# One core, delta rule plus gated feed-forward: grams 7, 10 and 11, a mask and the weight parts in other places of the order

## The chip, the cores and the metric

The program runs on one core of one Trainium2 chip, in one launch. Its time is the device time in microseconds (us); where several runs are given, it is their median. Times inside an execution are counted from the first instruction of the profiled one. The five engines are called PE (matrix multiplies, with PEld for its weight loads), DVE (vector), ACT (scalar), POOL and SP; SP and POOL issue most of the DMAs.

## The reference

Two stages stand behind each other. The first is a delta rule over 768 tokens for 4 batches and 8 heads of width 48:

```
for t in range(S):
    kt, vt, bt = (k_n[:, :, t], v[:, :, t], beta[:, :, t, None])
    y[:, :, t] = np.einsum('bhd,bhde->bhe', q[:, :, t], state)
    v_old = np.einsum('bhde,bhd->bhe', state, kt)
    state = state + bt[:, :, :, None] * np.einsum('bhd,bhe->bhde', kt, vt - v_old)
```

`k_n` is k divided by its norm. The second stage takes y as tokens of width 384: `h = gelu(x @ w_in)` (1024 wide), halves u and v, v normalised over its 512 columns, mixed over the tokens by `w_sg`, gated with u, multiplied by `w_out` and added to x.

## The kernel before

The tokens are cut into 12 chunks of 64 per pair of batches. For each chunk c the kernel needs a gram (products of k with k and of k with q, PE, copied by ACT into the tile `gm`), the inverse of a triangular matrix made from it (tile `zl`), and then the chain of the chunk. The inverse is made for two segments of two chunks at once by `lanes(g)`: g=0 is segment 0, g=1 segment 1, g=2 segments 2 and 3, g=3 segments 4 and 5. The gram is stored to memory by four small DMAs (`gstore`, tile `gd`), loaded in another layout (`zload`, tile `zl`), and worked on by about two hundred small DVE instructions. The result is stored (`zstore`, tile `zd`) and fetched per chunk (`zfetch`, tiles `zk` and `z`).

The chain of a chunk runs in turns, listed in `TURNS` as pairs (chunk, feed-forward chunk): turn 0 is (0, -), turn 1 (1, -), turn 2 (2, 0), turn 3 (3, 1), turn 4 (-, 2), turn 5 (4, 3), then (5, 4) to (11, 10) and (-, 11). The index of the turn is `at`. In a turn PE does old0, own0, state0, old1, own1, state1 and gram; between them stand pieces of the feed-forward of another chunk (gate, values), and at the end the two corners of the next chunk, which need its `z` and, from DVE, `vprep` (L481) and `turned` (L442). old0 and old1 end in a DVE addition (L508), on which own0 and own1 wait.

The order on every engine is the order of the code (`manual_schedule`); each engine takes its list from the front. Only the long DVE work is spread: `bg` is a list of closures with estimated costs, and `tick` takes some off after each piece, by the share of the turn in `SHARE`. In `bg` stand the operations of `lanes` and the parts of the decoding of `w_in`: per piece k three parts, begin, middle and end (`b`, `t`, `e` below), on ACT (L582, L583, L593) and DVE (L584 to L600). A piece is loaded into one of three buffers `ut` by `win_load`; the end of piece 1 issued the load of piece 4.

In turns 0 and 1 no feed-forward stands beside the chain. There `fill` takes its places: gram 6 in turn 0, gram 7 in turn 1, each in two halves, after some empty places (`later_on`). After the second half of gram 7 come its stores, the loads of `zl` for segments 2 and 3, and `lanes(2)` is put into `bg`. In turn 4 grams 10 and 11 (`dense`) and their stores stand together near the turn's end; the loads of `zl` for segments 4 and 5 follow, and `lanes(3)` goes into `bg` after own1 of turn 5.

After turn 11 a second phase with dense matrix multiplies (L639 to L641 with `wsgh` and `wouth`) fills PE to the end.

Of the kernel before, what the change touches and what calls it, by code (L numbers as in the profile page):

```python
# [23 lines left out]
NCH = SEQ // T  # L24
# [6 lines left out]
NC = DM // P  # L31
# [10 lines left out]
N_LAST = 4  # L42
# [13 lines left out]
def delta_rule_gmlp_kernel(  # L56
# [13 lines left out]
    nc = tc.nc  # L70
# [61 lines left out]
    def load(q, tile, src):  # L132

        flat = tile.rearrange("p j t -> p (j t)") if len(tile.shape) == 3 else tile.rearrange("p i j t -> p (i j t)")
        q.dma_start(
            out=flat.rearrange("p (n x) -> p n x", x=src.shape[-1]), in_=src.rearrange("n p x -> p n x"))

    loads = [nc.sync]

    def kload(c):  # L140
        if c < NCH:
            load(loads[0], KD[c % N_2], kqT[c])
# [9 lines left out]
    def vload(c):  # L152
        if c < NCH:
            load(loads[0], V[c % N_2], vtok[c])

    bg, credit = [], [0.0]
# [73 lines left out]
    def gstore(c, queues):  # L230
        if c >= NCH:
            return
        s, c2 = c // 2, c % 2
        if c2 == 0:
            gdt[s] = dram.tile([2, 2, 2, NP, 32, 32], F32, name="gd", bufs=4)
        for half in range(2):
            for sd in range(2):
                r0 = 64 * sd + 32 * half
                queues[(half + sd) % len(queues)].dma_start(
                    out=gdt[s][half, sd, c2].rearrange("j s t -> s j t"),  # L240
                    in_=GM[c % N_M][r0:r0 + 32, :, 0, 32 * half:32 * half + 32],
                )
# [8 lines left out]
    def above(c):  # L251

        if c >= NCH:
            return
        m = GM[c % N_M][:, :, 1]
        nc.vector.tensor_tensor(out=m, in0=m, in1=later.unsqueeze(1).broadcast_to([P, NP, T]), op=ALU.mult)
# [20 lines left out]
    def gram(c):  # L277

        if c >= NCH:
            return [[]] * 4  # L280

        def phase(qd):
            st = {}
            js = slice(4 * qd, 4 * qd + 4)

            def step(h):
                if h == 0:
                    st["ps"] = bank().rearrange("p (j x t) -> p j x t", x=2, t=T)
                for sd in range(2):
                    kq = KD[c % N_2][OWN[sd], :, 4 * qd + h]  # L290
                    mm(st["ps"][TOK[sd ^ (qd // 2)], h], kq[:, 0], kq)

            def done():
                nc.scalar.copy(out=GM[c % N_M][:, js], in_=st["ps"])

            return step, done, 4

        return [[phase(qd)] for qd in range(4)]

    def zload(s):  # L300
        if s >= NSEG:
            return
        if s % 2 == 0:
            zsrc[0] = prep.tile([P, 2, 32, 32], F32, name="zl")
        nc.sync.dma_start(
            out=zsrc[0][:, s % 2], in_=gdt.pop(s).rearrange("a b c j s t -> (a b c j) s t"))
# [270 lines left out]
    def decode(raw, f, m, hv, lv):  # L577
        low, top = raw[:, :, 0], raw[:, :, 1]
        mf, ff, lowf = m.bitcast(F32), f.bitcast(F32), raw.bitcast(F32)[:, :, 0]

        def one():
            nc.scalar.activation(out=mf, in_=raw.bitcast(F32)[:, :, 1], func=AF.Abs)  # L582
            nc.scalar.copy(out=lowf, in_=low.bitcast(U32))  # L583
            nc.vector.tensor_scalar(  # L584
                out=f, in0=top, scalar1=3, scalar2=0x3FFFFFFF,
                op0=ALU.logical_shift_left, op1=ALU.bitwise_and)
            nc.vector.scalar_tensor_tensor(
                out=f, in0=top, scalar=-0x40000000, in1=f, op0=ALU.bitwise_and, op1=ALU.bitwise_or)

        def two():  # L590
            nc.vector.scalar_tensor_tensor(
                out=ff, in0=mf, scalar=LEAST, in1=ff, op0=ALU.is_ge, op1=ALU.mult)
            nc.scalar.copy(out=hv, in_=ff)  # L593
            nc.vector.tensor_scalar(out=m, in0=f, scalar1=-0x800000, scalar2=None, op0=ALU.bitwise_and)
            nc.vector.scalar_tensor_tensor(
                out=lowf, in0=lowf, scalar=2.0 ** -52, in1=mf, op0=ALU.mult, op1=ALU.mult)

        def three():
            nc.vector.tensor_tensor(out=ff, in0=ff, in1=hv.bitcast(F32), op=ALU.subtract)
            nc.vector.tensor_tensor(out=lv, in0=lowf, in1=ff, op=ALU.add)  # L600

        return one, two, three
# [7 lines left out]
    def win_load(k, q):  # L610
        raw = fw.tile([P, 2, ND, 2, T], F32, name="ut", bufs=3).rearrange("p a b c d -> p (a b c d)")
        raw = raw.bitcast(I32)
        q.dma_start(out=raw.rearrange("p (n x) -> p n x", n=2), in_=w_in[k].bitcast(I32).rearrange("n p x -> p n x"))
        wraw[k] = raw.rearrange("p (n x) -> p n x", x=2)

    def decode_win(k):
        kk, cols = PIECES[k]
        parts = []

        def begin():  # L620
            f = fw.tile([P, DH], F32, name="vg", bufs=4)
            m = fw.tile([P, DH], F32, name="vg", bufs=4)
            parts.extend(decode(
                wraw.pop(k), f.bitcast(I32), m.bitcast(I32), winh[:, kk, cols], winl[:, kk, cols]))
            parts[0]()

        def end():
            parts[2]()
            win_left.remove(k)
            if 4 <= k + 3 < 2 * NC:  # L630
                win_load(k + 3, loads[0])

        win_left.append(k)
        return [(begin, 1.1), (lambda: parts[1](), 1.9), (end, 1.4)]
# [181 lines left out]
        deal([k0], [k1])  # L816
        gstore(c, (nc.sync, nc.scalar))
    nc.scalar.dma_start(out=beta_l, in_=beta)
    (b0, t0, e0), (b1, t1, e1), *others = [decode_win(k) for k in range(2 * NC)]
    win = [b0, b1, t0, e0, t1]  # L820
    waiting = [e1]
    for begin, *rest in others:
        win += [begin, *waiting]
        waiting = rest
    win += waiting
    zload(0)
    for _ in range(N_EARLY):
        win.pop(0)[0]()
# [2 lines left out]
    def dense(c):  # L831
        g = gram(c)
        deal(g[0], g[2])
        deal(g[1], g[3])

    def values_of(c):
        q0, q1 = qgram(c)
        deal([q0], [q1])
# [23 lines left out]
    kload(6)  # L862
    for k in (2, 3):
        win_load(k, nc.sync)
    bg += lanes(1) + win
    above(0)
    vprep(0)
# [26 lines left out]
    for at, (c, f) in enumerate(TURNS):  # L894
        new = at + N_GRAMS if at <= N_LAST else NCH
        ch = chain(c, new if at > 1 else NCH) if c is not None else None
        fill = []

        def rest(g, new, at):
            deal(g[1], g[3])  # L900
            gstore(new, (nc.sync,))
            if at == 1:
                zload(2)
                zload(3)
                bg.extend(lanes(2))

        if at < 2:
            g = gram(new)
            later_on = [lambda: None] * (4 - 2 * at)
            fill = [*later_on, lambda g=g: deal(g[0], g[2]), lambda g=g, new=new, at=at: rest(g, new, at)]  # L910
        after = TURNS[at + 1] if at + 1 < len(TURNS) else (None, None)
        n = after[0]
# [3 lines left out]
        def spent(what, n=1):  # L916
            tick(per * n * COST[what])

        def does(name):
            if ch:  # L920
                ch[name]()
                spent(name)

        def feeds(name, *i):
            if ffn:
                getattr(ffn, name)(*i)
                spent(name, i[0] if name == "values" else 1)
            elif fill:
                fill.pop(0)()
# [6 lines left out]
        def unit():  # L936
            if units:
                units.pop(0)()

        def early():  # L940
            k = next((k for k, _ in TURNS[at + 1:] if k is not None), None)
            if k is not None and k not in zks and k // 2 in zds:
                zfetch(k, nc.sync)
# [24 lines left out]
            units = [v_unit] * NT  # L968
        if c is not None:
            vload(c + 1)  # L970
        kload(new + 1)
        does("old0")
        early()
        if n is not None:
            if n > 1:
                above(n)
# [2 lines left out]
        feeds("gate", 0)  # L979
        does("own0")  # L980
        unit()
        feeds("gate", 1)
        early()
        does("state0")
# [5 lines left out]
        does("old1")  # L990
        unit()
        feeds("values", 4)
        does("own1")
        if c == 4:
            bg.extend(lanes(3))
        if c is not None:
            tload(c + 1)
        if ch and n is not None and n not in zks:
# [18 lines left out]

        if n == 1:
            values_of(n)
            above(n)  # L1020
        if ch:
            ready()
            corner("corner_a")
# [6 lines left out]
            spent("turn")  # L1030
        does("gram")
        if at > 1:
            if not ch:
                dense(new)
            gstore(new, (nc.sync,))
            if at == N_LAST:
                dense(new + 1)
                gstore(new + 1, (nc.sync,))
        if ffn:
            feeds("values", 2)  # L1040
        if ch:
# [11 lines left out]
        if n == 4:  # L1053
            zload(4)
            zload(5)
        if f == NK - 1:
            bg.extend(norm(0))
        if c == NCH - 4:
# [120 lines left out]
```

## Time and profile before

| what | value |
|---|---|
| runs | 537.33, 535.11, 536.76 us; median 536.76 |
| the profiled execution | 534.14 us, span 532.4 us |
| granted clock, mean | 0.871 of full speed |
| busy | PE 438.7 us (82%), PEld 396.1, DVE 331.8 (62%), ACT 181.9, POOL 71.6 |
| chain that ended last | PE 62%, DVE 19%, DMA 8%, ACT 5%, issue 5% |

How to read it: a busy engine at the bottom of the chain counts only in the stretch where it is the last to be ready. The mean of PE, 82%, hides stretches with nothing on PE and a second phase without a gap. "Issue" is idle time for which the profile shows no releaser. The granted clock of PE has two levels, 1.2 GHz (0.5) and 2.4 GHz (1.0).

### The profile page before, as it was taken

The numbers are of one execution on the slowest core, as the hardware profiler recorded it, in microseconds if no ns is written. First come the engines' busy times: TensorE is split into PE (matmuls) and PEld (weight loads), VectorE is DVE, ScalarE is ACT, GpSimd is POOL, SyncE is SP. The second block draws the span as 40 slices with busy tenths as digits, with TensorE's granted clock in tenths as the row PEclk, the third lists the DMA queues.
The fourth block names the chain that finished last, engine by engine and source line by source line (L and its number), as shares of the span: only waits on it lengthen the run. The fifth ranks groups of instructions, "written<-read, shape, count | busy, mean of one in ns | idle before, by whom it ended". The sixth has DMA issues, their size and how long they took to land.

```text
span 532.4 us, 17771 instructions
## 1 busy us (share of the span) xinstructions
PE 438.7 (82%) x7679; PEld 396.1 (74%) x7679; DVE 331.8 (62%) x932; ACT 181.9 (34%) x411; POOL 71.6 (13%) x84
## 2 busy tenths in 40 slices
PE   4414674825979989899949998999998999999997
PEld 2413664815858878787748787888998999999996
DVE  2999968849992227889913458633699536623332
ACT  3323244423333534153324455544434212211110
POOL 2100010040010203011010110000034222322130
PEclk9577555556988979899988997999999999999999
DMA  7996799276194986574594779456937654244204
GB/s 183 262 225 146 177 292 274 39 194 173 52 269 143 281 226 151 151 245 121 185 234 108 229 188 252 129 169 184 289 120 205 189 155 136 74 148 149 78 12 133
DMA packets 109181, 92.79 MB, mean 174 GB/s; under 512 B 71600, under 2 KB 84848, under 8 KB 109104
## 3 DMA queue, kind: packets, MB, share of 16 engines
q1 hardware_dynamic: 99152, 69.41, 46.6%
q0 software_dynamic: 5600, 20.71, 14.2%
q10 hardware_dynamic: 4352, 1.54, 1.2%
q8 instruction: 60, 0.98, 0.8%
q14 instruction: 17, 0.14, 0.1%
HBM read 63.30 MB, written 28.34 MB: 172 GB/s over the span
## 4 chain that ended last, share of the span: by engine, by line
PE 62%; DVE 19%; DMA 8%; ACT 5%; issue 5%; SPq 1%; ACTq 1%; DVEq 0%
PE ps L82 19%; PE ps L639 12%; PE ps L641 11%; PE ps L640 11%; PE ps L675 8%; DVE ztmp L367 4%; DVE zl L374 3%; DMA vraw<-vD 2%; DMA z<-zd 2%; DMA ut<-w_in 1%; DMA zl<-gd 1%; DMA kd<-kqT 1%; PE ps L661 1%; DVE vraw L754 1%; DVE bs L687 1%
## 5 line engine op out<-in xcount | busy, mean ns | idle before, releaser
L82 PEld LDWEIGHTS ps<-s,kq 48*64 48x64 f32 x1408 | 54.6, 157 | 16.0 <-issue 8.9
L82 PE MATMUL ps<-s,kq 48*64 48x48 f32 x1408 | 61.2, 243 | 4.2 <-issue 2.9
L782 POOL TENSOR_TENSOR ga<-ga,uT 128x384 f32<-128x384 f32 x32 | 36.3, 1141 | 162.9 <-DVE ga L779 117.6
L82 PE MATMUL ps<-kd 48*64 48x128 f32 (+1 forms) x768 | 33.8, 321 | 25.0 <-DMA kd<-kqT 25.0
L367 DVE TENSOR_TENSOR ztmp<-zl 128x50 f32<-128x50 f32 (+22 forms) x208 | 53.6, 296 | 0.1
L374 DVE TENSOR_TENSOR zl<-zl,ztmp 128x50 f32<-128x50 f32 (+22 forms) x208 | 53.4, 295 | 0.0
L82 PEld LDWEIGHTS ps<-kd 48*64 48x64 f32 x768 | 29.5, 169 | 27.2 <-DMA kd<-kqT 14.9
L82 PE MATMUL ps<-v,z 64*64 64x48 f32 x768 | 35.2, 247 | 16.8 <-issue 6.4
L639 PE MATMUL ps<-xh,winh 128*128 128x256 f32 x144 | 47.5, 330 | 0.6 <-issue 0.6
L82 PEld LDWEIGHTS ps<-v,z 64*64 64x64 f32 x768 | 31.8, 161 | 18.3 <-issue 10.2
L640 PE MATMUL ps<-xl,winh 128*128 128x256 f32 x144 | 43.4, 302 | 1.8 <-DVE xl L665 1.0
L641 PE MATMUL ps<-xh,winl 128*128 128x256 f32 x144 | 43.1, 299 | 0.8 <-issue 0.8
L644 ACT CAST gh<-ga 128x384 fp32r<-128x384 f32 x32 | 16.4, 511 | 77.3 <-POOL ga L782 63.5
L687 DVE BATCH_NORM_STATS2 bs<-vg 128x6 f32<-128x512 f32 x24 | 16.6, 690 | 29.9 <-ACT vg L681 29.7
L645 DVE TENSOR_TENSOR gl<-ga,gh 128x384 fp32r<-128x384 f32 x32 | 18.1, 565 | 26.8 <-ACT gh L644 26.8
L82 PE MATMUL ps<-u,gm 64*64 64x48 f32 x768 | 32.5, 239 | 2.7 <-issue 2.1
L641 PE MATMUL ps<-wouth,gl 128*128 128x384 f32 x96 | 32.4, 340 | 1.5 <-DVE gl L645 1.5
L639 PE MATMUL ps<-wsgh,vnh 128*128 128x384 f32 x96 | 32.6, 340 | 0.1
L641 PE MATMUL ps<-wsgh,winl 128*128 128x384 f32 x96 | 32.5, 339 | 0.0
L639 PE MATMUL ps<-wsgh,winh 128*128 128x384 f32 x96 | 32.5, 339 | 0.0
L640 PE MATMUL ps<-wsgl,winh 128*128 128x384 f32 x96 | 32.5, 339 | 0.0
L640 PE MATMUL ps<-wsgl,vnh 128*128 128x384 f32 x96 | 32.5, 339 | 0.0
(122 smaller groups left out, 1070.2 us busy)
## 6 DMA issues: line engine op xcount, KB each, us to landing
kq<-kqT POOLq DMA_DIRECT2D x10, 896.0 KB, 9.0
uD<-ut SPq DMA_DIRECT2D x12, 512.0 KB, 6.2
vD<-vg SPq DMA_DIRECT2D x24, 256.0 KB, 4.5
vraw<-vD SPq DMA_DIRECT2D x48, 128.0 KB, 3.2
uT<-uD SPq DMA_DIRECT2D x8, 768.0 KB, 5.1
kd<-kqT SPq DMA_DIRECT2D x6, 896.0 KB, 9.3
xD<-x SPq DMA_DIRECT2D x12, 384.0 KB, 6.7
x<-xD SPq DMA_DIRECT2D x48, 96.0 KB, 2.6
```

The lines of the kernel that those rows point to most:

```text
L82: return nc.tensor.matmul(out=out, lhsT=lhsT, rhs=rhs, start=start, stop=stop, skip_group_check=True)
L367: tv.tensor_tensor(out=st["tmp"][:, at:at + (r1 - r0) * w].rearrange("p (r t) -> p r t", t=w), in0=z[:, a, r0:r1, i:i + 1].broadcast_to([P ...
L374: tv.tensor_tensor(out=z[:, a, r0:r1, i + 1:32], in0=z[:, a, r0:r1, i + 1:32], in1=st["tmp"][:, at:at + (r1 - r0) * w].rearrange("p (r t) ...
L639: nc.tensor.matmul(out=ps, lhsT=sh, rhs=mh, start=(first and i == 0), stop=False)
L640: nc.tensor.matmul(out=ps, lhsT=sh, rhs=ml, start=False, stop=False)
L641: nc.tensor.matmul(out=ps, lhsT=sl, rhs=mh, start=False, stop=(last and i == n - 1))
L644: nc.scalar.copy(out=hi, in_=src)
L645: nc.vector.tensor_tensor(out=lo, in0=src, in1=hi.bitcast(F32), op=ALU.subtract)
L661: nc.tensor.transpose(out=ps[:, cc], in_=x[:, cc * P:(cc + 1) * P], identity=ident)
L675: nc.tensor.matmul(out=self.ps, lhsT=(self.xl if k == 2 else self.xh)[:, cc, bi], rhs=(winl if k == 1 else winh)[:, cc, DH:], start=(i == ...
L687: nc.vector.bn_stats(out=bs, in_=self.vg[bi])
L782: nc.gpsimd.tensor_tensor(out=gv, in0=gv, in1=uT[:, :, d], op=ALU.mult)
```

## The change

No arithmetic changes; instructions move.

- Turn 1: no empty places before gram 7; its halves stand after old0 and after own0 (before: after state0 and after old1). Its stores, the loads of `zl` and `lanes(2)` move with it.
- The mask of chunk 1 (`above(1)`, DVE L256) moves from the end of turn 0 to turn 1, behind old0.
- The parts of the `w_in` pieces come in another order: the end of piece 1 is done before the turns, the load of piece 4 is issued at the start of turn 0 and not by that end, and later ends stand ahead of the next middle part.
- Turn 4: gram 10 with its stores stands behind the first gate, gram 11 behind the second group of values (before both near the end). The k of chunk 11 is loaded at the end of turn 3 rather than at the start of turn 4.
- `lanes(3)` goes into `bg` at the end of turn 4, not after own1 of turn 5.

```
-            if 4 <= k + 3 < 2 * NC:
+            if 5 <= k + 3 < 2 * NC:
                 win_load(k + 3, loads[0])
...
+    win = [b0, b1, t0, e0, t1, e1, b2, t2, b3, e2, t3, b4, e3, t4, b5, e4, t5, e5]
...
     for k in (2, 3):
         win_load(k, nc.sync)
+    win.pop(0)[0]()
     bg += lanes(1) + win
...
-            later_on = [lambda: None] * (4 - 2 * at)
+            later_on = [lambda: None] * (4 - 4 * at)
...
-        kload(new + 1)
+        if at < N_LAST:
+            kload(new + 1)
+        if at == 0:
+            win_load(4, loads[0])
         does("old0")
         early()
+        if c == 1:
+            above(c)
...
+        if at == N_LAST:
+            dense(new)
+            gstore(new, (nc.sync,))
         feeds("gate", 1)
...
         feeds("values", 4)
+        if at == N_LAST:
+            dense(new + 1)
+            gstore(new + 1, (nc.sync,))
         does("own1")
-        if c == 4:
-            bg.extend(lanes(3))
...
+            if at == N_LAST - 1:
+                kload(NCH - 1)
...
             zload(4)
             zload(5)
+            bg.extend(lanes(3))
```

ACT in turn 1, before. `gm7` is the tile of gram 7; L582 and L583 begin a weight piece, L593 is in its middle part.

```order
L582 ACTIVATE vg_1265<-ut_1149 128x512
L583 CAST ut_1149<-ut_1149 128x512
L543 COPY s1_110<-ps_117 112x384
L558 COPY x_1303<-ps_1227 128x384
L593 CAST winh_69<-vg_1189 128x512
L294 COPY gm7_101<-ps_1312 128x512
L294 COPY gm7_101<-ps_1315 128x512
L593 CAST winh_69<-vg_1264 128x512
L294 COPY gm7_101<-ps_1354 128x512
L294 COPY gm7_101<-ps_1357 128x512
```

The same place now, from the first copies of gram 7:

```order
L294 COPY gm7_101<-ps_1229 128x512
L294 COPY gm7_101<-ps_1232 128x512
L530 COPY u_106<-ps_1252 128x384
L593 CAST winh_69<-vg_1192 128x512
L582 ACTIVATE vg_1289<-ut_1148 128x512
L583 CAST ut_1148<-ut_1148 128x512
L294 COPY gm7_101<-ps_1294 128x512
L294 COPY gm7_101<-ps_1297 128x512
L543 COPY s1_110<-ps_117 112x384
L558 COPY x_1359<-ps_1249 128x384
```

The last copies of gram 7 stood behind the middle part of piece 5; now they stand behind the middle part of piece 4 and the beginning of piece 5.

DVE at the start of turn 5, before: the corner's work for chunk 4, the two additions of its turn (L508), then the first instruction of `lanes(3)` (L322), which reads the loaded `zl`.

```order
L442 STREAM_TRANSPOSE ztk<-zk 128x256
L508 TENSOR_TENSOR v_107<-v_107,ps 128x384
L256 TENSOR_TENSOR gm_99<-gm_99,later 128x16x64
L508 TENSOR_TENSOR v_107<-v_107,ps 128x384
L322 COPY d_2864<-zl 128x64
L175 TENSOR_SCALAR rsq_y_2865<-d_2864 128x64
```

Now:

```order
L442 STREAM_TRANSPOSE ztk<-zk 128x256
L508 TENSOR_TENSOR v_107<-v_107,ps 128x384
L322 COPY d_2681<-zl 128x64
L175 TENSOR_SCALAR rsq_y_2682<-d_2681 128x64
L180 SCALAR_TENSOR_TENSOR rsq_t_2683<-d_2681,rsq_y_2682 128x64
L256 TENSOR_TENSOR gm_99<-gm_99,later 128x16x64
...
L346 SCALAR_TENSOR_TENSOR nb_2680<-nb_2680,beta_l 128x64
L508 TENSOR_TENSOR v_107<-v_107,ps 128x384
L351 TENSOR_TENSOR zl<-zl,nb_2680 128x1024 x2
```

The second addition of turn 5 now stands behind the first 16 instructions of `lanes(3)`.

SP in turn 4, before: `gd` of `gm_96` and `gm_97` are the stores of grams 10 and 11, `zl` the loads that read them.

```order
L239 DMA gd<-gm_95 32x16x32 x4
L682 DMA vD_73<-vg 128x512
L701 DMA uD_75<-ut 128x2x512
L682 DMA vD_73<-vg 128x512
L239 DMA gd<-gm_96 32x16x32 x4
L239 DMA gd<-gm_97 32x16x32 x4
L682 DMA vD_73<-vg 128x512
L305 DMA zl<-gd 128x1024 x2
```

Now:

```order
L239 DMA gd<-gm_95 32x16x32 x4
L682 DMA vD_73<-vg 128x512
L239 DMA gd<-gm_96 32x16x32 x4
L239 DMA gd<-gm_97 32x16x32 x4
L701 DMA uD_75<-ut 128x2x512
L682 DMA vD_73<-vg 128x512 x2
L305 DMA zl<-gd 128x1024 x2
```

The stores moved ahead of two feed-forward stores; all of these still stand ahead of the loads.

## Rows read from the trace of the kernel before

**Rows 1.** The page's second part: granted clock in 40 slices of 13.3 us.

```profile
PEclk9577555556988979899988997999999999999999
```

**Rows 2.** Busy time by stretch: length, then PE, PEld, DVE, ACT, POOL, clock, DMA, GB/s.

```profile
109.60:123.40 13.80, 0.02 (x4) 0.06 (x5) 9.50 (x22) 0.48 (x1) 6.00 (x7) 0.50 0.74 194
...
113.29:156.31 43.02, 27.58 (x697) 23.34 (x697) 42.13 (x134) 13.60 (x30) 8.87 (x11) 0.78 0.56 156
...
270.30:277.50 7.20, 0.02 (x1) 0.05 (x2) 1.40 (x2) 0.85 (x5) 0.00 (x0) 0.85 1.13 242
...
230.20:235.00 4.80, 4.80 (x146) 3.76 (x145) 3.78 (x10) 3.74 (x12) 0.00 (x0) 1.00 0.98 288
...
277.48:284.42 6.94, 6.94 (x146) 5.46 (x148) 1.99 (x4) 3.00 (x7) 0.00 (x0) 0.66 0.60 222
```

**Rows 3.** Waits at turn 1's and turn 8's ends: who, for whom, us, times, longest.

```profile
PE ps L82 <- DVE zl L356: 13.8, 1, 13.8
...
PE ps L82 <- DMA z<-zd: 7.2, 1, 7.2
```

**Rows 4.** DVE in time: start, us, instruction, shapes, [idle before <-releaser].

```profile
84.81 1.01 DVE L665 TENSOR_TENSOR xl<-ps,xh 128x384 fp32r<-128x384 f32 x2
...
91.39 0.55 DVE L508 TENSOR_TENSOR v<-v,ps 128x384 f32<-128x384 f32 x1
...
93.65 1.22 DVE L256 TENSOR_TENSOR gm<-gm,later 128x1024 f32<-128x1024 f32 x1
...
99.09 0.69 DVE L599 TENSOR_TENSOR vg<-vg,winh 128x512 f32<-128x512 f32 x1
...
113.29 0.22 DVE L322 COPY d<-zl 128x64 f32<-128x64 f32 x1 [8.80 <-DMA zl<-gd]
...
156.31 0.55 DVE L508 TENSOR_TENSOR v<-v,ps 128x384 f32<-128x384 f32 x1
```

**Rows 5.** ACT in time, turn 1.

```profile
94.66 0.68 ACT L582 ACTIVATE vg<-ut 128x512 f32<-128x512 f32 x1
...
102.01 0.62 ACT L593 CAST winh<-vg 128x512 fp32r<-128x512 f32 x1 [2.05 <-DVE vg L591]
102.53 1.06 ACT L294 COPY gm<-ps 128x512 f32<-128x512 f32 x2
```

**Rows 6.** SP's DMA issues in time; the us are those of issuing.

```profile
103.62 1.90 SPq L239 DMA_DIRECT2D gd<-gm  x4
...
183.60 2.69 SPq L701 DMA_DIRECT2D uD<-ut  x1
...
186.89 6.92 SPq L239 DMA_DIRECT2D gd<-gm  x8
...
194.38 1.72 SPq L305 DMA_DIRECT2D zl<-gd  x2
...
262.20 0.32 SPq L419 DMA_DIRECT2D zd<-zl  x1
```

**Rows 7.** The tile zl: its two loads in turn 1, then the two in turn 5.

```profile
DMA to landing us min/median/max: 3.9/5.0/6.1
...
DMA to landing us min/median/max: 4.7/5.7/6.7
```

**Rows 8.** DVE in time, turns 5 to 7.

```profile
201.94 0.56 DVE L508 TENSOR_TENSOR v<-v,ps 128x384 f32<-128x384 f32 x1 [6.64 <-PE ps L82]
202.60 0.22 DVE L322 COPY d<-zl 128x64 f32<-128x64 f32 x1
...
208.79 0.95 DVE L481 TENSOR_TENSOR v<-v,nv 128x768 f32<-128x768 f32 x1
...
216.41 0.55 DVE L508 TENSOR_TENSOR v<-v,ps 128x384 f32<-128x384 f32 x1
...
249.32 0.95 DVE L481 TENSOR_TENSOR v<-v,nv 128x768 f32<-128x768 f32 x1
```

**Rows 9.** Groups by form in lanes(2): instruction, count, busy us, mean ns, idle before.

```profile
L374 DVE TENSOR_TENSOR zl<-zl,ztmp 128x150 f32<-128x150 f32 x4 | 1.0, 302 | 0.0
```

More of the change, by code (lines that the diff above doesn't have):

```diff
@@ L818, in delta_rule_gmlp_kernel @@
     nc.scalar.dma_start(out=beta_l, in_=beta)
[L819 to L825, printed above, removed]
+    (b0, t0, e0), (b1, t1, e1), (b2, t2, e2), (b3, t3, e3), (b4, t4, e4), (b5, t5, e5) = (
+        decode_win(k) for k in range(2 * NC))
+    win = [b0, b1, t0, e0, t1, e1, b2, t2, b3, e2, t3, b4, e3, t4, b5, e4, t5, e5]
     zload(0)
@@ L1019, in delta_rule_gmlp_kernel @@
             values_of(n)
-            above(n)
         if ch:
@@ L1032, in delta_rule_gmlp_kernel @@
         if at > 1:
[L1033 to L1038, printed above, removed]
+            if ch:
+                gstore(new, (nc.sync,))
+            if at == N_LAST - 1:
+                kload(NCH - 1)
         if ffn:
```

## The prediction

> **What bounds the kernel now.** I read the granted clock by slices first, then busy time by stretch where the clock is low, then the waits there, then the engine queues in time. The clock line is low in two places: slices 4 to 8, about 50 to 130 us, and slice 20, at 270 us [rows 1]. There the reader should see what kind of wait it is, not PE's mean. Between 109.6 and 123.4 PE works 0.02 us, and DVE is busy 9.5 of 13.8 [rows 2]; the wait of 13.8 is put down to a `zl` instruction of DVE [rows 3]. DVE itself stood 8.8 us for the load of `zl` until 113.29 [rows 4], which reads the stores that SP issued at 103.62 [rows 6], which waited for ACT's last copy of gram 7, 102.53 + 1.06 = 103.59 [rows 5]. So turn 2 starts when gram 7 has gone gram, copy, store, load, DVE. From 113.29 to the L508 at 156.31 DVE is busy 42.1 of 43.0 us while PE has 27.6 [rows 2, 4]: there DVE is the bound, and what starts this block earlier moves all of it. The second place is turn 8: PE has nothing for 7.2 us until 277.5 [rows 2], waiting for the DMA of `z` of chunk 8 [rows 3], whose inverse DVE had ready only for the store at 262.20 [rows 6]. In most of the remainder PE is nearly full, so an instruction that moves there without a wait is worth nothing.
>
> All numbers below are in the profiled execution (534.14 us, a span of 532.4 and 1.7 around it), which lies 2.6 below the median of the runs, 536.76. I apply the sum to the median.
>
> **Part 1: gram 7 and the weight parts in turn 1.** The addition that frees own0 came at 91.39, behind a weight part that had waited for the load of piece 4. That load now goes out at the start of turn 0 and is no wait. But in DVE's new order the two subtractions `xl` (L665, 84.81, 1.01 together) [rows 4] stand ahead of nine weight operations of at most 0.69: 84.81 + 1.0 + 9 x 0.69 = 92.0, less for those that are shorter, and up to 1.4 more because the end of piece 1 (two of 0.69) now lies in the full DVE stretch ahead of turn 0. I take 91.7: no gain at own0. The first half of gram 7 fills PE while it waits there.
>
> From 91.7 DVE has the addition 0.55, two weight operations 1.38, two masks 2.44 (the moved one included) and the first operation of the next middle part 0.69 [rows 4]: 96.8. Then ACT does L593 0.62, two weight operations of about 0.68, and the two copies 1.06 [rows 5]: 99.8 against 103.59, or 3.8 earlier. From SP's issue at 103.62 to DVE's start took 9.7 us [rows 4, 6]. The two loads took 3.9 to 6.1 to land [rows 7]; the following x store and z fetches still depend on the end of turn 1 and now come after them, so I take 0.6 off: the block starts 4.4 earlier. In DVE's order seven more small `zl` operations stand ahead of the L508 at 156.31; one costs some 0.2 to 0.25 (four of a middle shape are 1.0 busy [rows 9]), together 1.4. **Gain 3.0.** Bounds: 0, if the copies still come behind a late weight load, and 5.5, if the loads land at their fastest. PE stays idle for about 10 of the 13.8 us, so the first low stretch of the clock remains.
>
> **Part 2: lanes(3) ahead of the second addition of turn 5.** This is a new wait. At 201.94 the addition came as soon as PE was done, with DVE idle for 6.64 us before it, and `lanes(3)` began behind it at 202.60 [rows 8]. Now L322 stands ahead of it and needs the loads of `zl`, issued from 194.38 to 196.1, the later one landing after some 4.7 us, the earlier after 6.7: about 201 [rows 6, 7]. What brings them forward: the eight stores of grams 10 and 11, issued from 186.89, now take the place of a feed-forward store issued at 183.60 [rows 6], 3.3 us earlier. That gives t = 197.5 for L322. Behind it stand 16 instructions, 202.60 to 208.79 = 6.2 us, and a mask 1.2 [rows 4, 8]: the addition at 204.9 in place of 201.94. In this turn own0's work is untouched; queued behind the waiting L322 are that addition (own1 waits for it) and then the corner's two operations for chunk 5. In turn 6, between L322 and the first addition, 13.8 us before [rows 8], now stand another mask, another addition (0.55) and 27 more small `zl` operations of 0.25 [rows 9]: 13.8 + 1.2 + 0.55 + 6.8 = 22.3, so 219.8 against 216.41. **Loss 3.3**; what DVE is ahead by then is spent in its later idle time. Bounds: 0, if the loads land by 194, and 6.9, if they land at 201 as now. The gap of PE may also drop its clock to 1.2 GHz; in turn 6 DVE sets the pace anyway, so I take nothing for it, at most the 2.2 of the next part.
>
> A rule speaks against even this. At 183 to 194 eight stores take 6.92 us to issue, 0.87 each, against 1.90 for four, 0.48 each, in turn 1 [rows 6]: they queue behind transfers in flight. The Trainium skill ("DMA: Bandwidth & Descriptors", "Issuing engines are not separate DMA queues") says that transfers of every issuing engine run on the same 16 DMA engines and interleave. By that rule the same bytes would stand ahead of the loads as before, and changing their order gives nothing; it is the first rival below.
>
> **Part 3: the wait in turn 8.** `lanes(3)` now ends ahead of the first addition of turn 8: its last scaling follows directly on the corner's two operations at the end of turn 7, 249.32 before [rows 8], 252.6 with the loss of part 2; the larger of those is 0.95, the other smaller, and the scaling has the shape of the mask, 1.22 [rows 4], in all some 2.6, so the store goes at about 255.2 and not at 262.20. From the store to PE's start took 277.5 - 262.2 = 15.3 us [rows 2, 6]: `z` is there by 270.5, and PE gets there at 270.3 + 3.3 = 273.6. The wait of 7.2 goes, with 3 us to spare. Its clock comes back too: the same 146 instructions take 6.94 us at a mean clock of 0.66 behind the wait and 4.80 at 1.0 two turns earlier [rows 2], 2.1 to 2.2. **Gain 9.4.** Bounds: 7.2 without the clock, and less if `z` is late again (a rival).
>
> **At nothing.** Grams 10 and 11 are the same PE work in the same turn; k of chunk 11 keeps its place among POOL's transfers, and if it landed after gram 11 starts PE would wait at most a few us in turn 4, which is in the bound of part 2. The moved mask of chunk 1 is 1.2 us on DVE, where DVE stood before. The end of piece 1 costs turn 0 up to 1.4, covered by turn 1's wait for the first addition, and counted there.
>
> Sum: -3.0 + 3.3 - 9.4 = -9.1. Profiled execution 525.0; on the median 536.76 - 9.1 = **527.7**.
>
> **Rivals.**
> 1. The loads of turn 5 land no earlier (the DMA engines are full). t = 201, loss 6.9, sum -5.5: 531.3. For it: the slow issue of the eight stores. Against it: these stores start earlier and two feed-forward stores come behind.
> 2. Turn 1 gives nothing: load 5, issued near 89, or ACT's queue holds the copies until 103.6. Sum 0 + 3.3 - 9.4 = -6.1: 530.7. For it: the copies still have two weight operations ahead of them. Against: 3.8 us of slack.
> 3. The change does not do what it says: DVE is so full in turns 5 to 7 that the inverse is late again and `z` comes 7 us later than I reckon, so that half of the wait stays (-4.7 and no clock gain lost): -3.0 + 3.3 - 4.7 = -4.4, 532.4; with the wait whole, 536.5.
> 4. Slower. One mechanism: L322 holds DVE's queue in turn 5 until `zl` lands. The loss grows one for one with t, and equals the gains at t = 194.2 + 12.4 = 206.6; at 212, when stores and loads together took twice as long as now, the loss is 17.8 and the time 536.76 + 5.4 = 542.2. For it: every DMA of that stretch is issued with waits. Against: nothing is added to the bytes ahead of the loads, which landed at 201.
>
> **How the numbers follow.** Chances: forecast 0.58, rival 1 0.15, rival 2 0.12, rival 3 0.09, rival 4 0.06. The forecast's own range, from the bounds of parts 1 and 2: 523.5 to 531.5. Rivals 1 and 2 lie inside its upper end; rival 3 partly outside. 8 in 10: 522.5 to 533.5. What a measurement can tell from no change is 0.5%, 2.7 us here. Faster by more: the forecast nearly whole, rivals 1 and 2 and half of rival 3, 0.82. Within: 0.11. Slower: 0.07.
>
> **What would show it.** Part 1: the copies of gram 7 done at 99 to 101, L322 of `lanes(2)` at 108 to 110, PE's gap some 3 us shorter. Part 2: a DVE wait on L322 of `lanes(3)` near 197 and a gap of PE of 2 to 4 us ahead of own1 of turn 5. Part 3: no PE wait for `z` in turn 8 and the clock at 1.0 through it. I am wrong if `zl` lands before 195 or after 203 on the old time scale, if PE still waits for `z` of chunk 8, or if the gain of turn 1 is lost before turn 4.

## The result, and the profile after

The changed kernel takes 528.83 us (median of 4 runs, 528.21 to 530.12), the kernel before 536.41 in the same session: a ratio of 0.9864, 95% interval 0.9835 to 0.9892. The prediction said 527.7. A second comparison gave 0.9891 (0.9849 to 0.9934). The time came out near the forecast, but not from the terms that I added up. Single executions of one kernel lie 1 to 2% apart in these sessions, and the traces of three that took longer as a whole (the second one of the changed kernel, 567.46 us, `lanes_late` and `turn1_loads_sp`) are left out of the means below. The profiled execution takes 528.21 us, with a span of 526.5, against 534.14 and 532.4.

The granted clock by slices (13.2 us each) and the row of PE's instruction queue on the page after:

```profile
PEclk9975566657999989999898998999999999999999
...
q8 instruction: 60, 0.98, 0.8%
```

The first low stretch is still there [rows 1]. Around turn 8 slices 20 and 21 were low before (8 tenths, counted from 0), now 19 and 21. In time DVE, then ACT, then SP's issues:

```profile
83.64 1.20 DVE L665 TENSOR_TENSOR xl<-ps,xh 128x384 fp32r<-128x384 f32 x2 [2.32 <-ACT xh L662]
...
90.09 0.56 DVE L508 TENSOR_TENSOR v<-v,ps 128x384 f32<-128x384 f32 x1
...
106.26 0.22 DVE L322 COPY d<-zl 128x64 f32<-128x64 f32 x1 [3.76 <-DMA zl<-gd]
...
190.62 0.22 DVE L322 COPY d<-zl 128x64 f32<-128x64 f32 x1 [2.11 <-DMA zl<-gd]
...
192.17 2.29 DVE L256 TENSOR_TENSOR gm<-gm,later 128x1024 f32<-128x1024 f32 x1
...
197.94 0.55 DVE L508 TENSOR_TENSOR v<-v,ps 128x384 f32<-128x384 f32 x1
```

```profile
94.88 0.62 ACT L593 CAST winh<-vg 128x512 fp32r<-128x512 f32 x1 [0.84 <-DVE vg L591]
...
96.54 1.07 ACT L294 COPY gm<-ps 128x512 f32<-128x512 f32 x2
```

```profile
97.63 1.90 SPq L239 DMA_DIRECT2D gd<-gm  x4
...
183.87 1.25 SPq L305 DMA_DIRECT2D zl<-gd  x2
...
248.75 0.59 SPq L419 DMA_DIRECT2D zd<-zl  x1
```

The copies of gram 7 end at 97.61 and not at 103.59 [rows 5], DVE starts `lanes(2)` at 106.26 and not at 113.29 [rows 4]. In turn 5 the inverse starts at 190.62 and not at 202.60 [rows 8], and the last store of the inverse goes out at 248.75 and not at 262.20 [rows 6]. Busy time by stretch (length, PE, PEld, DVE, ACT, POOL, clock, DMA, GB/s): PE's gap ahead of turn 2, DVE's stretch from L322 to the addition in chunk 3, and three stretches in turns 8 and 9.

```profile
108.12:117.65 9.53, 0.00 (x1) 0.03 (x1) 9.03 (x28) 0.48 (x1) 4.44 (x6) 0.50 0.94 230
106.26:150.50 44.24, 29.04 (x734) 24.55 (x723) 43.40 (x140) 15.50 (x37) 8.87 (x11) 0.78 0.60 161
257.99:265.57 7.58, 7.58 (x111) 5.86 (x107) 0.55 (x1) 1.09 (x3) 0.02 (x1) 0.55 0.20 31
255.90:257.62 1.72, 0.00 (x1) 0.00 (x0) 0.00 (x0) 0.00 (x0) 0.00 (x0) 1.00 0.78 166
275.69:277.88 2.19, 0.00 (x1) 0.01 (x1) 1.69 (x3) 0.00 (x0) 0.00 (x0) 1.00 0.67 203
```

The gap ahead of turn 2 is 9.5 and not 13.8 us [rows 2]. PE's waits from 240 to 350 us, as who, for whom, us, times, longest:

```profile
PE ps L82 <- issue: 6.1, 4, 1.9
PE ps L641 <- issue: 3.7, 4, 2.2
```

There is no wait for `z` any more [rows 3]; "issue" had 4.2 us in the same turns before, and now has 10.0 (0.2 of them ahead of L640). Three of these waits, in PE's time:

```profile
257.62 0.24 PE L82 MATMUL ps<-u,kt 64*48 64x48 f32 x2 [1.73 <-issue]
...
277.88 0.39 PE L641 MATMUL ps<-xh,winl 128*128 128x256 f32 x1 [2.19 <-issue]
...
303.32 0.25 PE L82 MATMUL ps<-u,kt 64*48 64x48 f32 x2 [1.02 <-issue]
```

Behind the first PE runs at a mean clock of 0.55 for 7.6 us (the third stretch above); the prediction had named a clock of 1.0 through turn 8. Behind the second it is 0.68 for 140 matmuls. To find where the time came from I compare the start of the same matmul, by its number in PE's order, in the two executions. The lead of the new kernel is 5.7 us at the start of turn 2, 4.6 at turn 5, 3.4 at own0 of turn 6, 5.0 at turn 8, 1.2 just ahead of the old place of the wait for `z`, 10.6 behind it, 7.0 a little later, and 5.9 at the end. So turn 1 gave 5.7, turn 5 took 1.2, turns 2 to 4 and 6 and 7 together gave 0.5, and what stands behind turn 8's start gave 0.9 net, where I had put 9.4.

### The profile page after: what moved, and what is told of

It reads as the page before. It is cut to its first block, busy times and chain, and to the rows that moved or that the text cites. A ratio compares the mean times of both kernels' runs of the same rounds, so it can differ in the third digit from the quotient of the medians.

```text
span 526.5 us, 17775 instructions
## 1 busy us (share of the span) xinstructions
PE 438.7 (83%) x7679; PEld 394.2 (75%) x7679; DVE 331.4 (63%) x932; ACT 181.9 (35%) x411; POOL 72.1 (14%) x84
## 4 chain that ended last, share of the span: by engine, by line
PE 60%; DVE 21%; DMA 7%; issue 6%; ACT 4%; SPq 1%; ACTq 0%; DVEq 0%
PE ps L82 17%; PE ps L639 12%; PE ps L641 11%; PE ps L640 11%; PE ps L675 8%; DVE ztmp L367 4%; DVE zl L374 4%; DMA vraw<-vD 2%; DMA zl<-gd 2%; DVE gm L256 1%; DMA uD<-ut 1%; DVE rsq_t L180 1%; PE ps L661 1%; DMA kd<-kqT 1%; DVE zl L351 1%
## 5 line engine op out<-in xcount | busy, mean ns | idle before, releaser
L82 PEld LDWEIGHTS ps<-s,kq 48*64 48x64 f32 x1408 | 53.0, 153 | 18.5 <-issue 11.0
L82 PE MATMUL ps<-s,kq 48*64 48x48 f32 x1408 | 59.7, 239 | 5.8 <-issue 4.1
L82 PE MATMUL ps<-kd 48*64 48x128 f32 (+1 forms) x768 | 37.8, 349 | 24.5 <-DMA kd<-kqT 23.6
L82 PEld LDWEIGHTS ps<-kd 48*64 48x64 f32 x768 | 32.6, 190 | 27.3 <-DMA kd<-kqT 14.2
L82 PE MATMUL ps<-v,z 64*64 64x48 f32 x768 | 33.7, 241 | 14.5 <-issue 7.8
L641 PE MATMUL ps<-xh,winl 128*128 128x256 f32 x144 | 42.4, 294 | 3.7 <-issue 3.7
L640 PE MATMUL ps<-xl,winh 128*128 128x256 f32 x144 | 42.7, 296 | 1.0 <-DVE xl L665 0.7
L82 PEld LDWEIGHTS ps<-v,z 64*64 64x64 f32 x768 | 30.4, 156 | 16.0 <-issue 8.2
L82 PE MATMUL ps<-u,gm 64*64 64x48 f32 x768 | 32.8, 238 | 3.4 <-issue 2.8
L508 DVE TENSOR_TENSOR v<-v,ps 128x384 f32<-128x384 f32 x22 | 12.0, 544 | 35.0 <-PE ps L82 35.0
L82 PEld LDWEIGHTS ps<-u,gm 64*64 64x64 f32 x768 | 29.3, 152 | 5.8 <-issue 3.7
L641 PE MATMUL ps<-wouth,gl 128*128 128x384 f32 x96 | 32.4, 340 | 0.8 <-DVE gl L645 0.8
L639 PE MATMUL ps<-wouth,gh 128*128 128x384 f32 x96 | 32.4, 340 | 0.3 <-ACT gh L644 0.3
L640 PE MATMUL ps<-wsgl,vnh 128*128 128x384 f32 x96 | 32.5, 339 | 0.0
```

What stands on the lines that cost most here:

```text
L82: return nc.tensor.matmul(out=out, lhsT=lhsT, rhs=rhs, start=start, stop=stop, skip_group_check=True)
L508: nc.vector.tensor_tensor(out=v[:, js[e]], in0=v[:, js[e]], in1=ks[e], op=ALU.add)
L639: nc.tensor.matmul(out=ps, lhsT=sh, rhs=mh, start=(first and i == 0), stop=False)
L640: nc.tensor.matmul(out=ps, lhsT=sh, rhs=ml, start=False, stop=False)
L641: nc.tensor.matmul(out=ps, lhsT=sl, rhs=mh, start=False, stop=(last and i == n - 1))
```

## The experiments

Leads below are such differences to the one profiled execution of before; times are ratios to runs of before on the same chip. By times, 2 us are not told apart here.

**Each part alone.** My theory after the traces: turn 1 is worth more than I had said, and the end of the wait for `z` is given back at once. The rival: the prediction's own sizes.

```
turn1_only: turns 3 to 5 as before     turn4_only: turn 1 and the weight parts as before
```

> Only the part in turn 1 (gram 7 early, mask of chunk 1, order of the weight parts, load of piece 4). Reading of the two traces: turn 2 starts 5.7 us earlier and keeps that to turn 8, where PE still waits about 7 us for z of chunk 8: 5 to 6 us below before, about 531. The sizes of the prediction instead: 3.0 below before, about 533.4. If both sizes are off, the start of turn 2 tells.

> Only the part in turns 3 to 5 (grams 10 and 11, k of chunk 11, lanes(3) early). The sizes of the prediction: +3.3 in turn 5 and -9.4 in turn 8, 6.1 below before, about 530.3. Reading of the traces: turn 5 loses under 1 us, the wait for z in turn 8 goes, but PE meets waits with no releaser there and runs at half clock, and most of the 9.4 is given back: 1 to 3 us below before, 533.5 to 535.5.

`turn1_only` came to 0.9867 (0.9803 to 0.9932), `turn4_only` to 0.9990 (0.9949 to 1.0031). The part in turn 1 makes the whole difference; the other makes none that can be measured. In `turn4_only` both of its mechanisms are there. DVE waits for `zl` in turn 5 and delays the addition, and PE waits 2.5 us for it ahead of own1:

```profile
199.84 0.22 DVE L322 COPY d<-zl 128x64 f32<-128x64 f32 x1 [3.80 <-DMA zl<-gd]
...
207.16 0.55 DVE L508 TENSOR_TENSOR v<-v,ps 128x384 f32<-128x384 f32 x1
...
207.76 0.26 PE L82 MATMUL ps<-v,z 64*64 64x48 f32 x2 [2.52 <-DVE v L508]
```

and the wait for `z` is gone; from 232 to 312 us this is the longest entry of PE's waits:

```profile
PE ps L82 <- issue: 4.0, 3, 2.0
```

The same two kernels' difference once more, on one chip:

> The changed kernel once more, beside its parts on one chip. 6 to 8 us below before; as turn1_only within 2 us if the part in turns 3 to 5 is worth nothing, 3 to 6 us below it if that part still gives what the prediction put on it.

> The part in turn 1 once more, for the comparison on one chip: 4 to 7 us below before.

0.9891 (0.9849 to 0.9934) for the change, 0.9883 (0.9823 to 0.9944) for its part in turn 1 alone: not told apart. The profiled execution of the part in turn 1 still has the wait of turn 8:

```profile
PE ps L82 <- DMA z<-zd: 6.5, 2, 5.7
```

**lanes(3) late again**, all else as changed.

```
         does("own1")
+        if c == 4:
+            bg.extend(lanes(3))
...
-            bg.extend(lanes(3))
```

> The changed kernel with lanes(3) put behind own1 of turn 5 again. If the early place of lanes(3) is what takes the wait for z of chunk 8 away, the inverse ends some 7 us later and PE waits 2 to 5 us for z in turn 8: 529 to 533. If the early stores of grams 10 and 11 alone do it, no wait for z, and turn 5 gains 0.5 to 1: about 528.

0.9908 (0.9868 to 0.9947), median 530.71. Its profiled execution has waits for `z` again, about as long as without the part:

```profile
PE ps L82 <- DMA z<-zd: 7.9, 2, 6.8
```

So the early place of `lanes(3)` is what takes the wait away, not the early stores alone. In time it is not told apart from the changed kernel.

**Whose waits are those called issue?** PE executes 7679 matmuls and as many weight loads. Queue 8 moved 60 packets, 0.98 MB (the row above): 16 KB each, one for about 256 PE instructions. I read the start of each packet in the trace, and what PE did then: each wait of over 0.25 us with no releaser from turn 7 to 11 in the changed kernel, save that ahead of L82 at 322.02, ends 2.3 to 3.0 us after a packet started, and they stand 126 to 128 matmuls (with their weight loads 252 to 256 instructions) or a multiple of that apart. For the wait at 277.88 the packet started at 275.52, for that at 257.62 at 255.35. My theory: PE stands because its next block of instructions comes late. The rival: the waits belong to places in the code. The test moves the edges of the blocks against the code, by n extra small matmuls early on (n is 32, 64 or 128).

```
+    for _ in range(n):
+        nc.tensor.matmul(out=warm[:, 0:32], lhsT=busy[:, 0:P], rhs=busy[:, 0:32], start=True, stop=True)
```

> The changed kernel with 32 small extra matmuls (64 PE instructions, 32 columns each) in PE's idle time at 10 to 22 us, their results unused. Theory: PE's instructions come in blocks of 256, and PE stands where a block's packet is late; the edges of the blocks now lie 32 matmuls earlier in the code, and the waits without a releaser in turns 7 to 11 move there or vanish; the time may change by up to 5 us either way (524 to 534). Rival: these waits belong to places in the code; they stay where they are, and the time is 528.8.

> As with 32, but 64 extra matmuls: half a block. Theory: the waits ahead of L641 and in the u,kt group of turns 8 to 11 are gone and others may stand 64 matmuls earlier in the code; 524 to 534. Rival: same places, 528.8.

> As with 32, but 128 extra matmuls: one whole block. Theory: the edges lie at the same places of the code again, one block number later, and so do the waits: within 1 us of 528.8. If the extra matmuls themselves matter (clock, an early delay), it differs from 528.8 by more, in the first 30 us.

The waits moved with the edges. PE in time with 32, with 64, and with 128 extra matmuls:

```profile
252.39 1.24 PE L82 MATMUL ps<-s,kq 48*64 48x48 f32 x27 [1.78 <-issue]
...
274.17 1.01 PE L82 MATMUL ps<-s,kq 48*64 48x48 f32 x27 [1.49 <-issue]
```

```profile
250.59 0.38 PE L82 MATMUL ps<-j,ztk 32*32 32x32 f32 x22 [1.67 <-issue]
...
272.66 0.45 PE L82 MATMUL ps<-j,ztk 32*32 32x32 f32 x23 [1.78 <-issue]
```

```profile
259.35 0.28 PE L641 MATMUL ps<-xh,winl 128*128 128x256 f32 x1 [2.10 <-issue]
...
305.78 0.25 PE L82 MATMUL ps<-u,kt 64*48 64x48 f32 x2 [1.41 <-issue]
```

The number of the matmul behind four of the waits, counted in the changed kernel's order (without the extra ones):

```
changed   4416   4925   5559   5942
n = 32    4384   4893   5527   5910
n = 64    4353   4861   5496   5878
n = 128   4416   4925   5559   5942   (at 4925 only 0.10 us)
```

32 less, 63 or 64 less, and the same again with one whole block. The rival falls. The times are 0.9891 (0.9849 to 0.9933), 0.9918 (0.9880 to 0.9956) and 0.9893 (0.9821 to 0.9966), not told apart: the waits change their places, and those of over 0.25 us at the edges from turn 8 on add up to 7.8, 7.6 and 5.8 us (7.9 in the changed kernel).

**Why does a packet start late?** The packet for a block starts when PE enters the block before it, if nothing stands in the way. In eight traces without extra matmuls (before, the changed kernel, `turn1_only`, `turn4_only`, `turn1_again`, `hold8`, `loads_sp` and `loads_sp_mid`, turns 0 to 11, 48 edges each) the 16 DMA engines were under 10% busy in the 3 us ahead of the packet at 46 edges: the packet started on the mean 0.3 us before PE entered the block ahead, and no such edge has a wait of over 0.25 us. At 128 edges the engines were at least 95% busy: the packet started 3.1 us after that moment on the mean (-0.8 to 6.6), and 60 of all 74 waits stand there. The Trainium skill ("Runtime: NRT & Kernel Launch", "Instruction fetch mechanics") says that instructions come in blocks of 16 KiB, 256 at a time, fetched while the block ahead is executed, and that crossing an edge is mostly hidden. The traces agree on the size and, at the 46 edges, on when the fetch begins; that it is hidden fails here at 74 of the 384 edges, none of them among the 46. Two experiments take transfers out of the way.

```
hold8, in turn 8 alone
-        if ffn:
+        if ffn and at != 8:
             ffn.ustore()
...
-            xstore(c)
+            if at != 8:
+                xstore(c)
...
             corner("corner_b")
+        if at == 8:
+            ffn.ustore()
+            xstore(c)
```

In `loads_sp` SP issues the loads of `kq` and `kt` in turns 5 to 11, and POOL, which issued them later in the turn before, no longer does. `tload` is changed as `qload`.

```
loads_sp
+    FROM = 4
...
-    def qload(c):
-        if c < NCH:
-            load(loads[0], KQ[c % N_2], kqT[c])
+    def qload(c, q=None):
+        if c < NCH and (q or c <= FROM):
+            load(q or loads[0], KQ[c % N_2], kqT[c])
...
         early()
+        if c is not None and c >= FROM:
+            qload(c + 1, nc.sync)
+            tload(c + 1, nc.sync)
```

> The changed kernel; in turn 8 alone the stores uD and xD are issued behind corner_b and not ahead of it. Theory: the wait of 2.19 us without a releaser ahead of L641 at 277.88 is PE waiting for its next block of instructions, whose packet started only at 275.52, behind the data of these stores. Then the packet starts 2 to 5 us earlier, the wait goes, and the half clock behind it: 525.5 to 527.5. Rival: that wait belongs to the place in the code or to PE's queue; it stays, and the time is 528.8.

0.9876 (0.9833 to 0.9920), median 528.66, and not the 525.5 to 527.5 expected. The wait at L641 is gone there, its packet started 3.5 us and not 6.0 after PE entered the block ahead. But in `turn4_only` it started 3.6 after that moment without any such edit, and PE did not wait either. So this one does not decide.

> The changed kernel; from turn 5 on the loads of kq and kt (1.3 MB a turn) are issued by SP behind the fetch of z at the turn's start, and no longer by POOL as soon as their tiles come free, about a turn earlier. Theory: PE's block packets start late when they come behind a burst of POOL's loads (v, kq and kt) and SP's stores at the turn's end; with the burst split the waits without a releaser ahead of L641 and in u,kt in turns 7 to 11 shrink from 7 us to under 3, and the half clock behind them goes: 522 to 526. Rivals: the waits are not tied to the transfers: 528 and the same waits; or the loads now come late themselves and PE waits for kq: over 530.

> The part in turn 1 with the same move of the loads. The wait for z of chunk 8 stays (about 6 us), the block waits shrink: 526 to 529. Against loads_sp it shows what the part in turns 3 to 5 gives once the block waits are smaller: 3 to 6 us by the theory.

`loads_sp`: 0.9872 (0.9823 to 0.9920), median 527.97, and not the 522 to 526 expected. The stretch from 250 to 300 us, and PE's waits from 236 to 299 (its lines stand one lower in the file, so that L641 here is L640 elsewhere):

```profile
250.00:300.00 50.00, 48.75 (x1332) 41.06 (x1332) 21.60 (x49) 23.38 (x62) 1.44 (x2) 1.00 0.74 212
```

```profile
PE ps L82 <- DVE v L509: 1.3, 1, 1.3
PE ps L641 <- DVE xl L666: 0.4, 1, 0.4
```

No wait called issue up to 298.7, the clock whole, and at the nine edges of these turns the packets started at most 2.0 us late. Here the lead went from -0.6 us at turn 8's start to +10.3 behind the old place of the wait: the 9.4 of the prediction, and 1.5 ahead of it, where before had two block waits of 1.1 us. That decides it for these turns: the gain is there, and late instruction blocks had taken it. Which transfers make a packet late is not shown: three of the nine packets started under 1 us late with engines as full. The kernel as a whole is no faster: a block wait of 3.5 us ends at 193.3 in turn 5, whose packet started at 190.5, before the moved loads of that turn were issued (192.93), and five more take 5.8 us from 300 us on. `turn1_loads_sp`, 0.9874 (0.9813 to 0.9935), is not told apart from it, where I had expected 3 to 6 us; so the gain of turn 8 shows in the trace and not in the times. The last run keeps the move to turns 6 to 9.

```
-    FROM = 4
+    FROM, TO = 5, 8
...
-        if c is not None and c >= FROM:
+        if c is not None and FROM <= c <= TO:
```

> As loads_sp, but kq and kt go by SP in turns 6 to 9 alone; turn 5 and turns 10 and 11 as in the changed kernel, since loads_sp had waits of 3.5 us there in turn 5 and of 2 to 5 us in turns 10 and 11. Theory: from turn 8 to turn 10 the gain of about 10 us as in loads_sp, without those waits: 523 to 526, below the changed kernel. Rival: executions differ so much in these waits that no difference to the changed kernel can be seen: 527 to 530.

0.9942 (0.9916 to 0.9969), median 530.03: a little worse than the rival said. The lead went from 2.2 to 12.5 us in turn 8, and was 6.2 by turn 10, where the waits came back:

```profile
PE ps L82 <- issue: 5.4, 4, 3.1
```

None of these versions beats the changed kernel. That a plan of all transfers against the edges of the blocks would, was not shown.

## Why the prediction was right, and where it was not

The time lay 1.1 us from the forecast, and that was luck: one part was too small, another too large. The gain was 7.6 us, 5.8 in the second comparison, for 9.1 forecast. By the means of the traces that have the term in question the parts are worth 4.9, -2.9 and 4.3 us: 6.3.

**Part 1, -3.0, was undersized.** The lead at turn 2 is 4.9 us on the mean (3.8 to 7.0 in nine traces with the same turn 1), 5.7 in the profile after, beyond the bound of 5.5. The step that failed is the start of own0's addition: I took the bound of nine weight operations of 0.69 as their value and added a delay from the end of piece 1, 91.7. The two subtractions came at 83.64, the nine operations took 5.3 us, and L508 stood at 90.09, 1.6 earlier than forecast; from there the chain ran in the order that I gave, DVE to 94.84 (96.8 forecast), ACT to 97.61 (99.8). From SP's issue to L322 took 8.6 us (9.1 assumed), and the stretch to chunk 3 grew from 43.02 to 44.24 [rows 2], 1.2 for the 1.4 that I had put on the small operations. The clock stayed low there, as said.

**Part 2, +3.3, held in size; its mechanism shows in part.** `zl` came earlier and L322 still waited 2.1 us. On the old scale L322 came at 190.62 + 4.6 = 195.2 in the profile after, and at 195.2 to 197.8 in the eight traces with the early `lanes(3)`, where I said 197.5. The work up to the addition took 7.3 us, 6.2 + 1.2 by the prediction. From turn 5 to own0 of turn 6 these eight lost 2.9 on the mean (1.2 to 4.2): 1.2 in the profile after, 4.2 in `turn4_only`. The gap of 2 to 4 us ahead of own1 is there in five of them, with 1.8 to 2.8 us; in the other three (0.25 us in the profile after) late instruction blocks had already delayed PE. `lanes_late`, without the early `lanes(3)`, lost 2.3 in that stretch beside two such waits of 3.6 us, so that not all of the 2.9 is shown to come from L322.

**Part 3, -9.4, failed as a net gain.** All of its own steps hold: the last store went out at 248.75, with a lead of 5 on the old scale 253.8 (255.2 forecast), and the wait of 7.2 is gone in every trace with the early `lanes(3)`. From the matmuls just ahead of its old place to those some hundred further on, the lead grows by 9.4 us in seven of these eight traces and by 8.8 in `loads_sp_mid`: the wait and its clock, as forecast. What failed is a term that the sum put at nothing without a reason: PE's other waits from turn 8 on, taken as unchanged. In the profile after, the lead falls from 5.0 to 1.2 ahead of that place, and from 10.6 to 5.9 behind it. The waits for instruction blocks from turn 8 on are 8.1 us there, 3.0 before (without the wait at 322.02, 328.96 before, which is not at an edge); 111 matmuls behind the first ran 7.1 us (4.5 before), 140 behind the second 5.4 (4.2). That is 9.4 - 5.1 - 2.6 - 1.2 = 0.5, beside the 0.9 measured. The low clock does not follow on every such wait: in `turn4_only` PE waited 2.0 us at the edge of the first, and ran the same 111 matmuls in 4.6 us at a clock of 1.0. On the mean of six traces (the two with moved loads left out) the part from turn 8's start is worth 4.3 (0.9 to 7.9), so with part 2 some 1.4 us, which the times of `turn4_only` (a gain of 0.5 us, -1.7 to +2.7) cannot tell from nothing.

Of the rivals, the first (L322 at 201) falls by L322 at 195.2 to 197.8, the second (nothing from turn 1) by `turn1_only`, the third (the wait for `z` stays) by its absence in every trace with the part, and the fourth (DVE held past 206.6) by L322 again. The one that was true is missing: another supplier of PE that takes the place of the wait removed. The profile of before showed it, in 4.2 us of waits called issue in those turns, and I read over them because they had no releaser. Three sums of the prediction are off: 219.8 - 216.41 is 3.4, rival 3 with the wait whole is 536.76 - 3.0 + 3.3 = 537.1 and not 536.5, and the bounds of parts 1 and 2 added to 527.7 give 521.9 to 534.3, wider than the range stated.

## What to carry to other kernels

When a wait of PE is taken away, ask what feeds PE next, its instructions too: look at waits without a releaser, and whether they come at a fixed count of instructions while the DMA engines are full. Run each part of a change alone: here one part made all of the gain that can be measured, and a total that agreed with the forecast hid it.

## What the runs showed of the hardware

The profile counts PE's instruction packets as a queue of the same 16 DMA engines that move the data (the row of queue 8), 16 KB for about 256 instructions, and a packet that starts under full engines is 3.1 us late on the mean. In the changed kernel PE went on 2.3 to 3.0 us after the start of a late packet (turns 7 to 11), and it stands where it uses the block ahead up before that: ahead of 277.88 it entered that block at 269.5, the packet started at 275.52, and PE was done with the block at 275.69. The Trainium skill ("DMA: Bandwidth & Descriptors", "Issuing engines are not separate DMA queues") says that transfers of all issuing engines share these engines; the late starts of the packets fit that for instructions as well. And the mask at L256 took 2.29 us in turn 5, against 1.22 [rows 4], while POOL worked on `zl` (2.29 also in `turn4_only`, `hold8` and `loads_sp` beside the same work, and 1.22 in turn 5 of `turn1_only`, where it stands apart from it):

```profile
190.91 2.50 POOL L324 TENSOR_SCALAR_AFFINE_SELECT zl<-zl 128x1024 f32<-128x1024 f32 x2 [20.50 <-DVE d L322]
```
